# Agent attention with a maxout network behind it: the first product moved ahead of the first scores, own orders for the last four groups, the last store in two halves

## The chip, the cores and the metric

One core of a Trainium2 chip. The metric is the device time of one execution of the kernel in microseconds (us), the median over several runs. The five engines of the core work side by side, each through its own list of instructions in order, and wait for each other by semaphores: PE (TensorE, matrix products; PEld is its loading of the stationary operand), DVE (VectorE), ACT (ScalarE), POOL (GpSimd) and SP (SyncE, which here only starts transfers). PE writes into PSUM, a small memory from which DVE and ACT fetch the results.

## The reference

`q`, `k` and `v` have 4 batches of 12,544 rows with 128 columns; `agents` has 4 batches of 49 rows. All inputs and the output are 32-bit floats.

```python
def _attn_ref(q, k, v, agents):
    scale = 1.0 / np.sqrt(q.shape[-1])

    def sm(a, b):
        s = scale * (a @ b.transpose(0, 2, 1))
        s = s - s.max(-1, keepdims=True)
        e = np.exp(s)
        return e / (e.sum(-1, keepdims=True) + 1e-09)
    a2k = sm(agents, k)
    agent_v = a2k @ v
    q2a = sm(q, agents)
    return (q2a @ agent_v).astype(np.float32)

def _moe_ref(x, w1, w2, w3, w_out):
    h = np.maximum(np.maximum(x @ w1, x @ w2), x @ w3)
    return (h @ w_out).astype(np.float32)
```

The second function gets the first one's result as 50,176 rows of 128 columns; `w1`, `w2`, `w3` are 128x768 and `w_out` is 768x128.

## The kernel before

**What is multiplied with what.** The agents gather from `k` and `v` a 49x128 matrix `agent_v` per batch. The kernel multiplies it with the differences `w2 - w1` and `w3 - w1` (and a linear remainder) once per batch. The result `G` has 49 rows (kept twice, on partitions 0 to 48 and 64 to 112) and 1,792 columns: 768 at `C21`, 768 at `C31`, and two times 128 at `C1O`, of which one is the linear part. After that a group of rows of `q` needs only its scores against the 49 agents and products with `G` and `w_out`.

**Two kinds of groups.** A k group takes nine tiles of 128 rows of `k` and `v` of one batch (`k_group`). The k groups of batch 0 run first, alone, in the start ("early"); those of the later batches are fitted in between the q groups. A q group (`q_group`) takes eight tiles of 128 rows of `q`; there are `NQ = 49` of them, numbered 0 to 48. The steps of q group `s`, by the names that the order uses:

- `qt`, `qe`: turn `q` so that its columns lie on partitions (by PE and a copy, or in the last batch by a transposing transfer from SP); `s`: scores on PE (L507); `ex`: their exponential on ACT (L513) into `e_q`; `ho`: a PSUM tile for small sums; `sum` (L521) and `rec` (L527): one over the row sums.
- For each of six blocks `f` of 128 hidden columns: `u` (L533, PE, product with the `C31` part of `G`), `a` (relu on ACT, L548), `v` (L533, PE, product with the `C21` part), `x` (maximum of both on DVE, L558, into the tile `r`). Block 3 (`FI`) differs: its relu stays in PSUM (L545), `v3` adds onto it, and `x3` is a relu on ACT (L556).
- For each half `o` of the group's rows: `lin` (L563, PE), then for every `f` the step `oc` (L572, PE, four matmuls of `r` with `w_out`), and `sc` (L579, DVE: the PSUM tile times one over the row sums, into `o_sb`). `oc13` is half 1, block 3.
- `store` (L586): one transfer of 512 KB from SP's queue, after both `sc`.

**The order is written by hand.** Every step is handed to `at` (L119) with a key, a number; `emit` (L125) sorts all steps by key and writes them out. A step whose needs are not yet written, or for which no buffer is free, is held back until they are. Every engine then runs its own instructions in exactly that order. A q group's keys are `6.0 * s` plus an entry of a table: `KEY` for groups while k groups are still mixed in, `LATE` for the groups of the last batch, `BORDER` and `BEGIN` around the change of a batch (L101). Large negative numbers in a table only mean "as soon as the needs allow".

**Rings.** PSUM is shared out as three tiles of two banks (`uv`: hidden products, transposes of `k`, the products that make `G`) and two of one bank (`om`: everything else). The step that takes a tile waits for the reader of the tile that had its place.

**The start.** After the last k group of batch 0, `k_tail(0, ...)` (L382) has DVE write `avT`, the normalised `agent_v` (L402, L403), and `product` (L408) multiplies it with `wall`, the weight differences, on PE (L421), 64 output partitions at a time, and copies the result into `G` on DVE (L426). For batch 0 the first call makes 256 columns from `C31` and, in the other bank of the same PSUM tile, the next 512; the second call makes the 768 columns from `C21` in another tile. A matmul into a tile waits for the copy that still reads from it. In the order before, the steps stand so: two matmuls that only keep PE busy (`keep_busy`), `s` and `ex` of group 0, both products, the transposes of group 0's k rows (L294, from a cast on POOL, L280), their copy (L300), `u0`, `u1`, fillers, `v0` and so on. The scores `s` of group 0 wait for ACT's copy of `qT` (L494).

Of the kernel before, what the change touches and what calls it, by code (L numbers as in the profile page):

```python
# [11 lines left out]
AF = mybir.ActivationFunctionType  # L12
# [4 lines left out]
def kernel(  # L17
# [18 lines left out]
    nc = tc.nc  # L36
    B, N, C = q.shape
# [3 lines left out]
    P = 128  # L41
    NF = Dff // P
    H = 64
# [52 lines left out]
        "oc11": 11.381, "oc13": 11.497,  # L96
    }
    PRODUCT_KEYS = (-8.717, -1.818)
    BEHIND = 2.6

    def table(s):  # L101
        if s + 1 in tails:
            return BORDER
        return BEGIN if s in tails and s < SB else KEY if s < SB else LATE
# [6 lines left out]
    def uv_tile(dtype=FP32):  # L111
        return psum.tile([P, 2, 512 if dtype == FP32 else 1024], dtype, tag="uv", bufs=3, name="uv_ps")
# [6 lines left out]
    def at(key, fn, name=None, needs=(), ring=None, frees=()):  # L119

        ops.append((key, len(ops), fn, name, needs, ring, frees))
# [258 lines left out]
    def k_tail(b, sum_key, keys, s):  # L382
        d = {}

        def reduce():
            w = KT // 2 * A
            t = Eacc[b]
            while w >= A:
                nc.gpsimd.tensor_tensor(out=t[:, :w], in0=t[:, :w], in1=t[:, w:2 * w], op=ALU.add)
                w = w // A // 2 * A  # L390
            nc.gpsimd.tensor_tensor(out=e_sum[:, :A], in0=t[:, :A], in1=t[:, KT * A - A:], op=ALU.add)

        def total():
            for h in range(2):
                nc.tensor.matmul(host[s][h * H:(h + 1) * H, :1], e_sum, ones[:, :1], start=True,
                                 stop=True, skip_group_check=True)

        def normalise():
            if s is None:

                r = last_tile["t"][:, :A]
                nc.vector.reciprocal(r, Vacc[b][:, A:])  # L402
                nc.vector.tensor_tensor(out=avT[:, b, :A], in0=Vacc[b][:, :A], in1=r, op=ALU.mult)  # L403
            else:
                nc.vector.reciprocal(r_ag[:, b:b + 1], host[s][:, :1])
            G[b] = work.tile([P, WC], BF16, tag="G", name="G")

        def product(c0, *ends):  # L408

            t = uv_tile().rearrange("p i c -> p (i c)")  # L410

            at0 = c0 if len(ends) == 1 else ends[0] - 512
            a = c0
            for z in ends:
                cuts = sorted({a, z} | {c for c in (at0 + 512, C1O) if a < c < z})
                for lo, hi in zip(cuts, cuts[1:]):
                    for h in range(2):


                        c = lo + (C if lo >= C1O and h == 0 else 0)  # L420
                        nc.tensor.matmul(t[h * H:(h + 1) * H, lo - at0:hi - at0], avT[:, b, :],  # L421
                                         wall[:, c:c + hi - lo], start=True, stop=True,
                                         skip_group_check=True)
                src = t[:, a - at0:z - at0]
                if s is None:
                    nc.vector.tensor_copy(out=G[b][:, a:z], in_=src)  # L426
                else:
                    nc.scalar.activation(G[b][:, a:z], src, AF.Copy, scale=r_ag[:, b:b + 1])
                a = z

        if s is not None:
            at(6.0 * (s - 1) + table(s - 1)["ke"] + 1.51, reduce, ("sum_e", b), [("kx", s - 1)])
            at(sum_key + 0.8, total, ("total", s), [("sum_e", b), ("ho", s)])
        at(sum_key + 0.81, normalise, ("normalise", b),
           [("ka", ("early", NT - last_size))] if s is None else [("total", s), ("ka", s - 1)])

        pieces = ((C31, C31 + 2 * P, C1O) if s is None else (C31, WC), (C21, C31))
        for i, piece in enumerate(pieces):
            at(keys[i], lambda piece=piece: product(*piece),
               ("product", b, i), [("normalise", b)], "uv", [("product", b, i)])  # L440


    def split(t0, t1, step):
# [10 lines left out]
    def q_group(s):  # L454
# [120 lines left out]
        def out_scale(o):  # L575
            if "out" not in d:
                d["out"] = work.tile([P, GT, C], FP32, tag="o_sb", bufs=3, name="o_sb")
            j, m = 2 * pairs[o][0], 2 * len(pairs[o])
            nc.vector.tensor_tensor(  # L579
                out=d["out"][:, j:j + m, :],  # L580
                in0=d["o", o].rearrange("p (j c) -> p j c", c=C),
                in1=d["r"][:, j:j + m].unsqueeze(2).to_broadcast([P, m, C]), op=ALU.mult)
# [53 lines left out]
        for o in range(2):  # L636
            put(f"lin{o}", lambda o=o: out_linear(o), ("ex", s), *new_linear, ring="om",
                frees=[(f"sc{o}", s)])
            for f in range(NF):
                put(f"oc{o}{f}", lambda o=o, f=f: out_hidden(o, f), (f"lin{o}", s), (f"x{f}", s))  # L640
            put(f"sc{o}", lambda o=o: out_scale(o), ("rec", s),
                *[(f"oc{o}{f}", s) for f in range(NF)], *([("store", s - 3)] if s >= 3 else []))
        at(key + 12.2, store, ("store", s), [("sc0", s), ("sc1", s)])

    def ramp():

# [22 lines left out]
    for g, n in enumerate(first_sizes):  # L669
        k_group(0, sum(first_sizes[:g]), n, first_key + 6.0 * g, None)  # L670

        if 4 <= g < len(first_sizes) - 3:
            fillers += [(first_key + 6.0 * g + 0.55, 3), (first_key + 6.0 * g + 1.3, 3)]
    k_tail(0, last_key, (last_key + 0.95, last_key + 1.02), None)
    for key, n in fillers + [(last_key + 0.9, 2), (KEY["u1"] + 0.01, 2),
                             (KEY["u3"] + 0.05, 2)]:
        at(key, lambda n=n: keep_busy(n), ("busy", key), (), "om", [("busy", key)])
# [45 lines left out]
```

## Time and profile before

| what | value |
|---|---|
| median of 3 runs | 463.16 us (463.14 to 463.19) |
| the profiled execution's own time | 462.84 us |
| its span, first to last instruction | 461.0 us |
| distance of the stores of groups 44, 45, 46 (issued at 431.44, 439.30, 447.16) | 7.86 us |
| last store: issued, landed | 457.46, 460.07 us |
| one maximum on DVE (L558), mean of 245 | 1.220 us |
| one relu on ACT (L548), mean of 245 | 1.027 us |
| one scaling on DVE (L579), mean of 98 | 0.688 us |
| one output matmul on PE (L572), mean of 2,352 | 0.220 us from start to end; the next one starts earlier |

All times inside the profile are in microseconds from the start of the span. A row of the timeline gives start, duration, engine, line, operation, the tiles `out<-in`, shapes, and in brackets how long the engine was idle before it and who released it. Matmuls overlap: a row of 24 matmuls that takes 1.50 us is 1.35 us of the chain, and the rest is the last one's way through the array. In the stretch from 436.6 to 444.4, which is steady, PE was busy 7.77 of 7.80 us, ACT 7.27 and DVE 7.23. In the last stretch, from 452.3 to 461.0, PE was busy 4.20 of 8.70, DVE 3.71 and ACT 0.15.

The profile covers one execution; the runs of the table are others of the same kernel.

### The profile page before, as it was taken

How to read it: one execution, taken by the hardware profiler on the slowest of the kernel's cores; microseconds unless marked ns; L12 is line 12 of the kernel's file. 1: busy time of each engine (PE TensorE's matmuls, PEld its weight loads, DVE VectorE, ACT ScalarE, POOL GpSimd, SP SyncE). 2: the span in 40 equal slices, each digit the busy share in tenths (PEclk: the TensorE clock that was granted, in tenths of full speed). 3: DMA queues.
4: the chain of work that ended last, by engine and by line, in shares of the span. 5: the costliest groups of instructions: out<-in, count | busy, mean ns of one | idle time of the engine just before them, and what ended most of it. 6: DMA issues, size and time to landing. Idle time of an engine off the chain costs nothing.

```text
span 461.0 us, 13320 instructions
## 1 busy us (share of the span) xinstructions
PE 436.1 (95%) x5457; PEld 273.5 (59%) x5462; DVE 402.2 (87%) x510; ACT 396.6 (86%) x460; POOL 171.6 (37%) x179
## 2 busy tenths in 40 slices
PE   2597899999999999999999999999999999999996
PEld 2465456666656666666656666666656555555554
DVE  3255899999989999999989999999988999999995
ACT  3365989899899899898998998999999999999982
POOL 3235964644362536445273355363240101100000
PEclk9999999999999999999999999999999999999999
DMA  8999999999998999988998999997766465644122
GB/s 327 408 410 392 345 346 354 337 342 255 310 315 286 286 261 339 286 268 248 276 351 268 287 314 291 279 280 180 167 151 178 129 198 149 176 122 125 60 94 91
DMA packets 82632, 118.53 MB, mean 257 GB/s; under 512 B 56391, under 2 KB 57867, under 8 KB 82571
## 3 DMA queue, kind: packets, MB, share of 16 engines
q1 hardware_dynamic: 82368, 117.59, 84.8%
q8 instruction: 42, 0.69, 0.6%
q14 instruction: 19, 0.16, 0.1%
q10 hardware_dynamic: 203, 0.10, 0.1%
HBM read 78.74 MB, written 25.69 MB: 227 GB/s over the span
## 4 chain that ended last, share of the span: by engine, by line
PE 81%; DMA 8%; DVE 5%; ACT 4%; issue 1%; SPq 0%; POOL 0%; DVEq 0%; ACTq 0%
PE uv_ps L533 34%; PE o_ps L572 29%; PE o_ps L563 6%; DMA st<-in_k_dram 5%; PE m_ps L486 4%; DVE r L558 4%; PE m_ps L507 3%; ACT a_sb L548 2%; DMA st<-in_q_dram 2%; DMA st<-in_v_dram 2%; PE m_ps L323 2%; PE m_ps L312 1%; PE m_ps L521 1%; DVE o_sb L579 0%; DVE G L426 0%
## 5 line engine op out<-in xcount | busy, mean ns | idle before, releaser
L558 DVE TENSOR_TENSOR r<-uv_ps,a_sb 128x1024 bf16<-128x1024 f32 x245 | 297.3, 1220 | 16.3 <-PE uv_ps L533 7.6
L548 ACT ACTIVATE a_sb<-uv_ps 128x1024 bf16<-128x1024 f32 x245 | 240.8, 1027 | 15.4 <-PE uv_ps L533 13.9
L533 PE MATMUL uv_ps<-e_q,G 49*128 49x512 bf16 (+3 forms) x1248 | 186.8, 368 | 2.6 <-DVE G L426 0.4
L572 PE MATMUL o_ps<-wo_bf,r 128*128 128x128 bf16 x2352 | 175.2, 220 | 0.2 <-DVE r L558 0.2
L572 PEld LDWEIGHTS <-r 128*128 128x128 bf16 x2352 | 137.8, 98 | 40.1 <-issue 38.1
L533 PEld LDWEIGHTS <-G 49*128 49x128 bf16 x1248 | 57.7, 93 | 64.7 <-issue 32.9
L342 POOL TENSOR_TENSOR Eacc<-Eacc,e_k 128x441 f32<-128x441 f32 (+1 forms) x30 | 30.5, 1015 | 124.9 <-ACT e_k L317 124.9
L579 DVE TENSOR_TENSOR o_sb<-o_ps,recips 128x512 f32<-128x512 f32 x98 | 67.5, 688 | 9.1 <-PE o_ps L572 6.3
L481 POOL CAST q_bf<-st 128x1024 bf16<-128x1024 f32 x49 | 51.0, 1043 | 62.0 <-DMA qT<-q_bf 59.2
L556 ACT ACTIVATE r<-uv_ps 128x1024 bf16<-128x1024 f32 x49 | 50.2, 1024 | 18.0 <-PE uv_ps L533 17.7
L280 POOL CAST k_bf<-st 128x1152 bf16<-128x1152 f32 (+2 forms) x45 | 50.4, 1120 | 28.6 <-DMA st<-in_k_dram 26.4
L545 ACT ACTIVATE uv_ps<-uv_ps 128x1024 f32<-128x1024 f32 x49 | 49.6, 1012 | 0.2
L563 PE MATMUL o_ps<-G,e_q 128*128 128x256 bf16 x196 | 38.0, 276 | 0.0
L287 POOL CAST v_bf<-st 128x1152 bf16<-128x1152 f32 (+1 forms) x33 | 37.5, 1136 | 0.9 <-ACT e_q L513 0.6
L513 ACT ACTIVATE e_q<-m_ps 128x512 bf16<-128x512 f32 x49 | 29.8, 608 | 0.5 <-PE m_ps L507 0.5
L285 ACT ACTIVATE v_bf<-st 128x1152 bf16<-128x1152 f32 (+1 forms) x12 | 12.9, 1074 | 13.9 <-DMA st<-in_v_dram 13.9
L563 PEld LDWEIGHTS <-e_q 128*128 128x128 bf16 x196 | 12.5, 97 | 18.7 <-issue 18.0
L300 DVE COPY kT<-uv_ps 128x1152 bf16<-128x1152 bf16 (+1 forms) x14 | 9.9, 708 | 14.8 <-PE uv_ps L294 14.8
L486 PEld LDWEIGHTS <-q_bf 128*128 128x128 bf16 x264 | 14.9, 98 | 13.0 <-issue 11.1
L492 DVE COPY qT<-m_ps 128x1024 bf16<-128x1024 bf16 x32 | 21.8, 680 | 0.0
L486 PE MATMUL m_ps<-ident,q_bf 128*128 128x128 bf16 x264 | 20.4, 220 | 0.4 <-POOL q_bf L481 0.4
L507 PE MATMUL m_ps<-qT,agT 128*64 128x512 bf16 (+3 forms) x104 | 19.9, 388 | 0.7 <-ACT qT L494 0.7
(71 smaller groups left out, 224.9 us busy)
## 6 DMA issues: line engine op xcount, KB each, us to landing
st<-in_q_dram SPq DMA_DIRECT2D x46, 512.0 KB, 5.2
out_dram<-o_sb SPq DMA_DIRECT2D x46, 512.0 KB, 3.8
st<-in_k_dram SPq DMA_DIRECT2D x40, 576.0 KB, 6.7
st<-in_v_dram SPq DMA_DIRECT2D x40, 576.0 KB, 7.9
st<-in_k_dram SPq DMA_DIRECT2D x3, 512.0 KB, 8.0
st<-in_v_dram SPq DMA_DIRECT2D x3, 512.0 KB, 6.8
wst<-in_moe_w_dram SPq DMA_DIRECT2D x3, 384.0 KB, 10.7
st<-in_q_dram SPq DMA_DIRECT2D x2, 384.0 KB, 4.9
```

Source lines behind the costliest of these rows:

```text
L280: nc.gpsimd.tensor_copy(out=d["kb"][:, :n, :], in_=d["k"][:, :n, :])
L287: nc.gpsimd.tensor_copy(out=d["vb"][:, :n, :], in_=d["v"][:, :n, :])
L481: nc.gpsimd.tensor_copy(out=d["qb"], in_=d["q"])
L486: nc.tensor.transpose(t[:, j * P:(j + 1) * P], d["qb"][:, j, :], ident)
L533: nc.tensor.matmul(t[:, h, j0 * P:j1 * P], G[b][h * H:h * H + A, col + f * P:col + (f + 1) * P], d["e"][h * H:h * H + A, j0 * P:j1 * P], s ...
L545: nc.scalar.activation(u, u, AF.Relu)
L548: nc.scalar.activation(a_sb[f], u, AF.Relu)
L556: nc.scalar.activation(r, v_ps[f], AF.Relu)
L558: nc.vector.tensor_tensor(out=r, in0=v_ps[f], in1=a_sb[f], op=ALU.max)
L563: nc.tensor.matmul(t[:, i * 2 * C:(i + 1) * 2 * C], d["e"][:, jj * P:(jj + 1) * P], G[batch[jj]][:, C1O:C1O + 2 * C], start=(i == 0), stop ...
L572: nc.tensor.matmul(t[:, c:c + C], r_sb[f][:, h, jj * P:(jj + 1) * P], wo_bf[:, f, :], start=False, stop=True, skip_group_check=True)
L579: nc.vector.tensor_tensor(out=d["out"][:, j:j + m, :], in0=d["o", o].rearrange("p (j c) -> p j c", c=C), in1=d["r"][:, j:j + m].unsqueeze( ...
```

## The change

Three things change. All else, and the order of groups 1 to 44, stays as it was.

1. The products of batch 0 come as three steps. The first makes 256 columns from `C31` (one PSUM tile, first bank). The second, in a tile of its own, makes the next 512 columns of `C31` and the first 512 of `C21`, with two copies. The third makes the last 256 columns of `C21` in the second bank of the first tile, so it waits for the first copy. The first two are keyed ahead of `s` of group 0, the third behind it. The products of batches 1 to 3 keep their two pieces.
2. Groups 45 to 48 get a table each (`LAST`) in place of `LATE`. As written out, the end of the lists then reads: on DVE `x4` of group 48, `sc0` of group 47, `x5` of group 48, `sc0` of group 48 (before: `x4`, `x5`, `sc0` of 47, `sc1` of 48, `sc0` of 48); on PE, behind `x5`, the steps `oc15`, `oc05`, `oc02`, four matmuls each (before: `oc15`, `oc13`, `oc12`, `oc11`, `lin0` and all six `oc0`).
3. Of group 48, the half `o = 1` is scaled on ACT, by four instructions of 128x128, and stored from ACT's queue; the half `o = 0` is scaled on DVE as before and stored from SP's queue. Each store is 256 KB, 2 KB per partition.

```diff
     PRODUCT_KEYS = (-8.717, -1.818)
+    LAST = [
...
+        {"a4": -135.5952, "s": -3.6850, "ex": -2.2030, "ho": -1.9346, "u0": -1.3390,
...
+         "oc05": 60.1508, "lin0": 70.3912, "oc03": 74.0752, "oc00": 92.6315, "oc01": 97.6449,
+         "x5": 102.3830, "oc02": 107.1067},
+    ]
     def table(s):
+        if s >= NQ - len(LAST):
+            return LAST[s - NQ]
...
+        def multiply(t, at0, a, z):
+            cuts = sorted({a, z} | {c for c in (a - at0 + 512, C1O) if a < c < z})
+            for lo, hi in zip(cuts, cuts[1:]):
+                for h in range(2):
+                    c = lo + (C if lo >= C1O and h == 0 else 0)
+                    nc.tensor.matmul(t[h * H:(h + 1) * H, at0 + lo - a:at0 + hi - a], avT[:, b, :],
+                                     wall[:, c:c + hi - lo], start=True, stop=True,
+                                     skip_group_check=True)
...
+        cut = C31 + 2 * P
+        def product_first():
+            t = d["p"] = uv_tile().rearrange("p i c -> p (i c)")
+            multiply(t, 0, C31, cut)
+            nc.vector.tensor_copy(out=G[b][:, C31:cut], in_=t[:, :cut - C31])
+        def product_second():
+            t = uv_tile().rearrange("p i c -> p (i c)")
+            multiply(t, 0, cut, C1O)
+            multiply(t, 512, C21, C21 + 512)
+            nc.vector.tensor_copy(out=G[b][:, cut:C1O], in_=t[:, :C1O - cut])
+            nc.vector.tensor_copy(out=G[b][:, C21:C21 + 512], in_=t[:, 512:])
+        def product_third():
+            multiply(d["p"], 512, C21 + 512, C31)
+            nc.vector.tensor_copy(out=G[b][:, C21 + 512:C31], in_=d["p"][:, 512:512 + C31 - C21 - 512])
...
+        if s is None:
+            at(keys[0], product_first, ("product", 0, 0), [("normalise", 0)], "uv", [("product", 0, 2)])
+            at(keys[0] + 0.001, product_second, ("product", 0, 1), [("product", 0, 0)], "uv",
+               [("product", 0, 1)])
+            at(keys[1], product_third, ("product", 0, 2), [("product", 0, 0)])
...
+            if s == NQ - 1 and o == 1:
+                for i in range(m):
+                    nc.scalar.activation(d["out"][:, j + i, :], d["o", o][:, i * C:(i + 1) * C], AF.Copy,
+                                         scale=d["r"][:, j + i:j + i + 1])
+                return
...
-        at(key + 12.2, store, ("store", s), [("sc0", s), ("sc1", s)])
+        def store_half(o):
+            queue = nc.scalar if o else nc.sync
+            j, m = 2 * pairs[o][0], 2 * len(pairs[o])
+            dst = out[s * GT * P:(s + 1) * GT * P, :].rearrange("(p j) c -> p j c", j=GT)
+            queue.dma_start(dst[:, j:j + m, :], d["out"][:, j:j + m, :])
+        if s < NQ - 1:
+            at(key + 12.2, store, ("store", s), [("sc0", s), ("sc1", s)])
+        else:
+            for o in range(2):
+                at(key + 120, lambda o=o: store_half(o), ("store", s, o), [(f"sc{o}", s)])
...
-    k_tail(0, last_key, (last_key + 0.95, last_key + 1.02), None)
+    k_tail(0, last_key, (last_key + 0.93, last_key + 1.02), None)
```

## The prediction

> **What bounds the kernel now.** I read the page's header and shares first, then the chain that ended last with its pieces in time, then the timeline of the two stretches that the diff touches.
>
> ```profile
> span 461.0 us, 13320 instructions
> ...
> PE 436.1 (95%) x5457; PEld 273.5 (59%) x5462; DVE 402.2 (87%) x510; ACT 396.6 (86%) x460; POOL 171.6 (37%) x179
> ...
> PE 81%; DMA 8%; DVE 5%; ACT 4%; issue 1%; SPq 0%; POOL 0%; DVEq 0%; ACTq 0%
> ```
>
> PE is the bound of the body. From 63 us to 445 us nearly every piece of the chain is a PE piece, and the SP rows issue the stores of groups 44, 45 and 46 at 431.44, 439.30 and 447.16, one group per 7.86 us. The change leaves the order of groups 1 to 44 alone, so there is nothing to gain in the body; a shift made before it arrives at its end. What can move lies at the two ends, where the chain leaves PE. The start first (pieces of the chain: start, us, what; then rows of the timeline):
>
> ```profile
> 42.08 1.03 ACT qT L494
> 43.11 0.04 issue
> 43.16 0.41 PE m_ps L507 x2
> 43.56 0.12 PE uv_ps L421 x2
> 43.69 0.02 issue
> 43.71 0.43 DVE G L426
> 44.14 0.04 issue
> 44.19 0.42 PE uv_ps L421 x2
> 44.61 0.02 issue
> 44.63 1.56 DVE G L426 x2
> 46.20 0.04 issue
> 46.24 0.39 PE uv_ps L533 x2
> ```
>
> ```profile
> 43.30 1.15 POOL L280 CAST k_bf<-st 128x1152 bf16<-128x1152 f32 x1 [1.94 <-DMA st<-in_k_dram]
> ...
> 44.85 0.68 PE L294 MATMUL uv_ps<-ident,k_bf 128*128 128x128 bf16 x9
> ...
> 45.46 0.39 PE L533 MATMUL uv_ps<-e_q,G 49*128 49x512 bf16 x2
> ...
> 45.89 1.94 ACT L548 ACTIVATE a_sb<-uv_ps 128x1024 bf16<-128x1024 f32 x2 [1.69 <-PE uv_ps L533]
> ```
>
> The product G, a PE and DVE ping-pong, begins only after the scores that wait for qT, although its operand avT is written at 42.34 (the DVE row of L403: 42.13 for 0.21). The second matmul of group 0 waits for the last copy into G until 46.24. Then the end:
>
> ```profile
> 451.67 2.36 DVE L558 TENSOR_TENSOR r<-uv_ps,a_sb 128x1024 bf16<-128x1024 f32 x2 [0.39 <-PE uv_ps L533]
> ...
> 454.08 1.07 PE L572 MATMUL o_ps<-wo_bf,r 128*128 128x128 bf16 x16 [0.21 <-DVE r L558]
> ...
> 455.20 1.50 PE L572 MATMUL o_ps<-wo_bf,r 128*128 128x128 bf16 x24
> 456.75 0.69 DVE L579 TENSOR_TENSOR o_sb<-o_ps,recips 128x512 f32<-128x512 f32 x1 [0.87 <-PE o_ps L572]
> ```
>
> Here the last r is done at 454.03, PE then has 40 output matmuls and a linear pair left, and one scaling and one store of 512 KB stand behind them. The store is issued at 457.46 and lands at 460.07.
>
> **The start, step by step.** Moved: the first product's two 256-column matmuls, before the scores. They need avT (42.34 + 0.05) and the fillers' end (42.48): start 42.48. The DVE copy followed such a pair by 0.34 (43.37 to 43.71), so it runs from 42.82 to 43.24. The second step has its own PSUM tile and four matmuls of 512 columns, two at a time, 0.21 a pair (44.19 to 44.40): it ends about 43.05, before qT at 43.10, so the scores start at 43.16 as now and the exponential at 43.60. DVE then copies 512, 512 and 256 columns instead of 512 and 768. Its rows are 0.42 for 256 and 1.55 for 512 and 768 back to back, so about 0.26 for each 256 more: 0.66, 0.66 and 0.42, until 45.0 instead of 46.19. The fourth copy instruction costs DVE 0.2 (2.16 against 1.97 in all), covered because DVE starts 0.89 earlier. The third product waits for the first copy (43.24); behind it on PE stand the transposes of group 0's k, which cannot start before POOL's cast is done anyway (43.30 + 1.15 = 44.45). So they start at 44.50, not 44.85: 0.35 earlier. The first hidden matmul follows 0.61 later (44.85 to 45.46): 45.11, and ACT's first relu at 45.54 against 45.89. DVE's first maximum gains more, about 0.85, because the second hidden pair no longer waits until 46.24.
>
> Which one counts is ACT: from 45.89 its rows run on to 49.49 with 0.14 us of idle time, so the later steps keep ACT's gain, not DVE's. What is late next is POOL (casts of the next groups end at 47.00 and 48.87), whose consumers on PE start at 48.08 and 50.62, so it has room for the shift. I take **0.35**. Ends: 0.2, if the third copy (until 45.0 plus its signal) and the first relu collide and half the gain goes; 0.55, if the shorter wait for the second transposes (they waited 0.54 for DVE, which gains more than ACT) is passed on. No SP or POOL instruction moves here.
>
> **The end.** The own tables put the last group's remaining work before its last maximum. In the new order DVE ends with maximum 4, scaling of group 47, maximum 5, one scaling of group 48; PE has three blocks of four matmuls left after maximum 5. From maximum 5 to the end of the last scaling, now: 457.44 - 454.03 = 3.41. Then: 0.05 to PE, 12 matmuls (1.07 for 16, less four at 0.056 from 1.35 for 24 = 0.85), 0.04, 0.69 = 1.63. Saved 1.78. Paid: group 47's scaling, 0.69, now stands ahead of maximum 5. Against it, DVE's idle rows before that point (0.37 at 445.24, 0.39 at 451.67) can close; maximum 5 still needs ACT's and PE's rows, both over 90% busy, so I close a third, 0.25. Net 1.78 - 0.69 + 0.25 = **1.35**. Ends: 1.85 with all 0.76 closed; 0.5 with none closed and a new stall like DVE's 0.57 before 455.19.
>
> ACT's scaling of the other half replaces one DVE instruction of 0.69 by four of 128x128. The nearest row is L240, 0.27 for 128x128, so 4 x 0.27 = 1.08. It starts after maximum 5 and the first of the three blocks (0.05 + 0.39 + 0.04) and is done at 1.56, beside DVE's 1.63: no cost while it ends first; if each took 0.4 as L249's 256 columns do, 0.45 later than DVE. On ACT nothing is behind it but its store; its queue of semaphore waits is for stores landed 14 us before (group 45's).
>
> **The store.** The last store took 2.60 us from issue to landing, and the five before 2.61 to 2.90. In the packet records its 128 packets of 4,096 bytes took 160 ns each, eight per DMA engine: 1.28, leaving 1.32 around it. 2,048-byte packets, as the halves make, took 84 ns: eight are 0.67. Alone, the last half would land in 1.99, gain 0.6. Together both halves take 1.32 + 1.34 = 2.66 from the first issue; with ACT's half issued 0.1 to 0.2 ahead that is **0.1** gained. Lower end -0.3: the one earlier issue on ACT's queue took 0.57 against 0.34 on SP's. That load was used 4.3 us after its issue, beside 4.04 for SP's load issued at the same moment, so the queue itself is not slow.
>
> [...]
>
> **Sum.** 0.35 + 1.35 + 0.1 = 1.8. The profiled execution took 462.84, of which 461.0 is span; 1.84 around it stays. So its span becomes 459.2 and its time 461.04. The median of the runs is 463.16, 0.32 above the profiled one; with the same difference the forecast is **461.36**.
>
> **Rivals.** (a) The start's gain is absorbed: transposes and relus are set by casts and loads that don't move. For it, POOL's idle 1.94 for a DMA before 43.30; against it, the 0.35 is counted from that very cast. Time 461.7. (b) The new orders of groups 45 to 48 lose between the groups what they save at the end: PE, DVE and ACT are 99%, 93% and 93% busy there, so an order that suits the end can leave PE waiting. For it, the trace's own irregular orders: over a border two groups took 17.87 us (stores at 132.11 and 149.98) against 16.70, so 1.17 more, of which 0.75 or so is product work. Losing one such 1.17 gives 463.16 - 1.8 + 1.17 = 462.5, no change by this measurement. (c) Slower: the same stall in three of the four groups, 3 x 1.17 = 3.5, gives 464.9; it decides from two groups on (1.8 / 1.17 = 1.5). Against both, the border orders have a product in them and these don't, and every instruction of these groups is one that the steady order has too.
>
> **How the numbers follow.** Forecast 0.68 (its own range 460.8 to 462.0), (a) 0.12, (b) 0.12, (c) 0.08. About 0.2%, 0.93 us, is what a measurement of this kernel can tell from no change. Forecast and (a) are faster by more, (b) within it, (c) slower: 0.80, 0.12, 0.08. The range: the upper ends of the three terms together are 3.0 and the lower 0.4; all three seldom fall together, so 2.6 to 0.7 saved, 460.6 to 462.5, which takes in (a) and touches (b).
>
> **What would show it.** Right: the first product matmul starts near 42.5, the first relu near 45.5, the body's chain 0.35 earlier (group 42's store near 415.4 instead of 415.72); the last DVE scaling ends near 455.75, 1.6 after the last L558; two store issues within 0.3 us, the last landing 2.3 to 2.6 after the first. Wrong: a body shifted by nothing or by over 0.6; group periods over 8 us after 430; ACT's four scalings ending well after DVE's; the ACT store landing later than 3 us after issue.

## The result and the profile after

| | before | after |
|---|---|---|
| median, on the same chip | 463.18 us (463.14 to 463.34, 4 runs) | 461.83 us (461.79 to 461.94, 4 runs) |
| ratio after to before | | 0.9971, 95% interval 0.9953 to 0.9988 |
| distance of the stores of groups 43 to 47 | 7.86, 7.86, 7.87, 7.48 us | 7.86, 7.86, 7.44, 6.49 us |
| last maximum ends, last scaling ends | 454.49, 457.90 us | 454.66, 456.31 us |
| last store issued, landed | 457.93, 460.54 us | 456.35, 459.05 us |

Faster by 1.35 us, 0.3%. The forecast was 461.36. The time rows of "before" are from a second profile of the unchanged kernel (463.26 in the median of its own runs, span 461.5), since the first profile turns out to be an early execution: the load of group 0's q lands at 40.27 us in it and at 40.67 in the second, and everything behind is 0.4 later. In the other twelve profiles of this study it lands between 40.53 and 40.81, in the changed kernel's at 40.53. Comparisons below are with the second profile, and the lines of the changed kernel stand 35 to 63 further down than before: L421 is L456, L280 is L320, L294 is L334, L533 is L590, L548 is L605, L558 is L615, L572 is L629 and L579 is L642.

The page of the changed kernel (span; busy time by engine; the chain's shares):

```profile
span 460.0 us, 13331 instructions
...
PE 436.4 (95%) x5462; PEld 273.9 (60%) x5462; DVE 401.4 (87%) x510; ACT 397.6 (86%) x464; POOL 171.5 (37%) x179
...
PE 82%; DMA 8%; DVE 3%; ACT 3%; issue 1%; POOL 0%; SPq 0%; DVEq 0%; ACTq 0%
```

PE still bounds the body. DVE's share of the chain falls from 5% to 3%: the ping-pong at the start and the scalings at the end are what went. The start, as pieces of the chain of waits (start, us, what):

```profile
42.30 0.43 PE m_ps L294 x2
42.73 0.66 PE uv_ps L456 x6
43.40 0.02 issue
43.41 0.42 PE m_ps L564 x2
43.84 0.07 issue
43.91 1.16 POOL k_bf L320
45.07 0.05 issue
45.11 0.68 PE uv_ps L334 x9
45.79 0.54 PE uv_ps L590 x4
```

The six product matmuls (L456) stand ahead of the scores (L564), and no copy into G is on the chain any more. In its place stands a piece that wasn't there: POOL's cast of k, then the transposes that need it. The end, as rows of the timeline:

```profile
452.85 0.68 DVE L642 TENSOR_TENSOR o_sb<-o_ps,recips 128x512 f32<-128x512 f32 x1
453.44 1.21 DVE L615 TENSOR_TENSOR r<-uv_ps,a_sb 128x1024 bf16<-128x1024 f32 x1
...
453.86 1.73 PE L629 MATMUL o_ps<-wo_bf,r 128*128 128x128 bf16 x28
455.18 1.14 ACT L639 ACTIVATE o_sb<-o_ps,recips 128x128 f32<-128x128 f32 x4 [2.19 <-PE o_ps L629]
455.62 0.69 DVE L642 TENSOR_TENSOR o_sb<-o_ps,recips 128x512 f32<-128x512 f32 x1 [0.96 <-PE o_ps L629]
456.34 0.33 SPq L710 DMA_DIRECT2D out_dram<-o_sb  x1
456.35 0.38 ACTq L710 DMA_DIRECT2D out_dram<-o_sb  x1
```

Only three blocks of four matmuls are left behind the last maximum; both scalings end at the same moment, and so both stores start at the same moment. Where the end's time came from is in the busy times of the stretch 445 to 453 us (length, then busy time and instructions of each engine, clock, DMA). First the unchanged kernel:

```profile
445.00:453.00 8.00, 7.53 (x79) 4.19 (x77) 7.19 (x9) 6.58 (x7) 0.00 (x0) 1.00 0.18 70
```

Then the changed one:

```profile
445.00:453.00 8.00, 7.97 (x99) 5.47 (x97) 7.44 (x10) 6.54 (x7) 0.00 (x0) 1.00 0.18 70
```

PE's work at the end is the same in both kernels; the new orders do 20 matmuls more of it before 453, so that less stands behind the last maximum.

### The profile page after: what moved, and what is told of

Its sections match the earlier page's. It is cut to its first block, busy times and chain, and to the rows that moved or that the text cites. A ratio compares the mean times of both kernels' runs of the same rounds, so it can differ in the third digit from the quotient of the medians.

```text
span 460.0 us, 13331 instructions
## 1 busy us (share of the span) xinstructions
PE 436.4 (95%) x5462; PEld 273.9 (60%) x5462; DVE 401.4 (87%) x510; ACT 397.6 (86%) x464; POOL 171.5 (37%) x179
## 4 chain that ended last, share of the span: by engine, by line
PE 82%; DMA 8%; DVE 3%; ACT 3%; issue 1%; POOL 0%; SPq 0%; DVEq 0%; ACTq 0%
PE uv_ps L590 35%; PE o_ps L629 30%; PE o_ps L620 6%; DMA st<-in_k_dram 5%; PE m_ps L543 4%; PE m_ps L564 3%; DVE r L615 3%; ACT a_sb L605 2%; DMA st<-in_q_dram 2%; DMA st<-in_v_dram 2%; PE m_ps L363 2%; PE m_ps L352 1%; PE m_ps L578 1%; ACT e_q L570 0%; ACT G L463 0%
## 5 line engine op out<-in xcount | busy, mean ns | idle before, releaser
L615 DVE TENSOR_TENSOR r<-uv_ps,a_sb 128x1024 bf16<-128x1024 f32 x245 | 297.1, 1219 | 16.8 <-PE uv_ps L590 7.8
L605 ACT ACTIVATE a_sb<-uv_ps 128x1024 bf16<-128x1024 f32 x245 | 241.1, 1027 | 14.0 <-PE uv_ps L590 12.6
L590 PE MATMUL uv_ps<-e_q,G 49*128 49x512 bf16 (+3 forms) x1248 | 186.9, 368 | 1.8 <-ACT a_sb L605 0.4
L629 PE MATMUL o_ps<-wo_bf,r 128*128 128x128 bf16 x2352 | 175.5, 220 | 0.0
L629 PEld LDWEIGHTS <-r 128*128 128x128 bf16 x2352 | 137.7, 98 | 40.7 <-issue 39.1
L590 PEld LDWEIGHTS <-G 49*128 49x128 bf16 x1248 | 57.9, 93 | 64.1 <-issue 32.1
L642 DVE TENSOR_TENSOR o_sb<-o_ps,recips 128x512 f32<-128x512 f32 x97 | 66.7, 688 | 8.5 <-PE o_ps L629 5.6
L320 POOL CAST k_bf<-st 128x1152 bf16<-128x1152 f32 (+2 forms) x45 | 50.5, 1121 | 29.1 <-DMA st<-in_k_dram 23.1
L334 PE MATMUL uv_ps<-ident,k_bf 128*128 128x128 bf16 x116 | 11.2, 255 | 9.8 <-POOL k_bf L320 8.5
```

Of the source, the lines that this page charges most:

```text
L320: nc.gpsimd.tensor_copy(out=d["kb"][:, :n, :], in_=d["k"][:, :n, :])
L590: nc.tensor.matmul(t[:, h, j0 * P:j1 * P], G[b][h * H:h * H + A, col + f * P:col + (f + 1) * P], d["e"][h * H:h * H + A, j0 * P:j1 * P], s ...
L605: nc.scalar.activation(a_sb[f], u, AF.Relu)
L615: nc.vector.tensor_tensor(out=r, in0=v_ps[f], in1=a_sb[f], op=ALU.max)
L629: nc.tensor.matmul(t[:, c:c + C], r_sb[f][:, h, jj * P:(jj + 1) * P], wo_bf[:, f, :], start=False, stop=True, skip_group_check=True)
L642: nc.vector.tensor_tensor(out=d["out"][:, j:j + m, :], in0=d["o", o].rearrange("p (j c) -> p j c", c=C), in1=d["r"][:, j:j + m].unsqueeze( ...
```

## The experiments

Some of these kernels start from the kernel before, the others from the changed one. Differences are always to the kernel before on the same chip, because its median was 463.19 to 463.43 on different chips.

### Each part alone

The unchanged kernel once more, as the yardstick:

> The kernel before unchanged, a second profile of it, to see how much of a difference between two profiles is chance. If the 0.3 us by which the first q load landed later in the changed kernel's profile, and the 0.4 us that its body lost between groups 8 and 24, are chance, then this profile differs from the first one by similar amounts, up to 0.4 us, at the start or in the body; if they belong to the changed kernel, this profile agrees with the first within 0.1 at every group.

Measured: 463.26 (463.17 to 463.45), ratio 1.0000 (0.9991 to 1.0009). The later landing of q is chance by it (40.67); the loss between groups 8 and 24 is the changed kernel's, for their exponentials are 135.58 apart there, and 135.25 here and 135.23 in the first profile.

Part 1 alone, the products in the start:

```diff
+            at(keys[0], product_first, ("product", 0, 0), [("normalise", 0)], "uv", [("product", 0, 2)])
+            at(keys[0] + 0.001, product_second, ...
+            at(keys[1], product_third, ("product", 0, 2), [("product", 0, 0)])
...
-    k_tail(0, last_key, (last_key + 0.95, last_key + 1.02), None)
+    k_tail(0, last_key, (last_key + 0.93, last_key + 1.02), None)
```

> The kernel before with only the products of batch 0 in three steps, two of them ahead of the first scores. Theory (the changed kernel's gain is nearly all at the end; at the start the first relu hangs on POOL's cast of group 0's k rows, and so on the landing of that load): 0.0 to 0.4 us saved, and in the profile the first relu follows the end of that cast by 1.1 us as it does in the changed kernel (45.06 to 46.16), with a group 1 exponential 0.1 to 0.4 earlier than in the kernel before. Rival (the product's place is worth the forecast 0.35 in every run and the profile of the changed kernel lost it by chance): 0.35 saved or a little more.

Measured: 462.67 (462.32 to 463.00), ratio 0.9988 (0.9979 to 0.9997), 0.58 less, more than the theory's 0.4. The first relu follows the cast's end by 1.09, as expected; group 1's exponential is 0.54 earlier, not 0.1 to 0.4. Where the 0.58 comes from is told further down.

Part 2 alone, the tables of the last four groups:

```diff
     def table(s):
+        if s >= NQ - len(LAST):
+            return LAST[s - NQ]
```

> The kernel before with only the own tables of groups 45 to 48; the last group is scaled on DVE twice and stored in one piece from SP. Theory (the order alone brings the end's gain, the scaling on ACT keeps it from being given back): maximum 5 ends about 0.7 later than before, then both scalings stand behind each other on DVE, so the last scaling ends 0.4 to 0.7 later than in the changed kernel: 0.7 to 1.1 us saved. Rival (ACT's scaling costs as much as it spares, 1.14 us on ACT against 0.69 on DVE): 1.3 to 1.5 saved.

Measured: 461.96 (461.79 to 462.17), ratio 0.9972 (0.9962 to 0.9982), 1.29 less, more than the theory's 1.1 and nearly the rival's 1.3: the last maximum ends only 0.32 later than before, not 0.7. DVE's two last scalings run back to back and end 1.80 after the last maximum instead of 3.41; the one store takes 2.61 to land.

Part 3 alone, ACT's scaling and the two stores, in the old order:

```diff
+            if s == NQ - 1 and o == 1:
+                for i in range(m):
+                    nc.scalar.activation(...)
...
+                at(key + 120, lambda o=o: store_half(o), ("store", s, o), [(f"sc{o}", s)])
```

> The kernel before with only the last group's half 1 scaled on ACT and the two half stores; order of the groups as before. In that order half 1 is done 1.5 us before half 0, so its store is under way when half 0 is done. Theory (the half store is worth something only if the halves are staggered): the last half store lands about 2.0 after its issue instead of 2.6, 0.5 to 0.7 us saved. Rival (two stores cost what one does, the fixed part decides): 0.0 to 0.2 saved.

Measured: 462.60 (462.49 to 462.78), ratio 0.9986 (0.9977 to 0.9995), 0.65 less. The rows show why this is much more than in the changed kernel:

```profile
455.71 1.14 ACT L620 ACTIVATE o_sb<-o_ps,recips 128x128 f32<-128x128 f32 x4 [2.74 <-PE o_ps L610]
455.73 1.50 PE L610 MATMUL o_ps<-wo_bf,r 128*128 128x128 bf16 x24
456.89 0.38 ACTq L691 DMA_DIRECT2D out_dram<-o_sb  x1
457.27 0.69 DVE L623 TENSOR_TENSOR o_sb<-o_ps,recips 128x512 f32<-128x512 f32 x1 [2.12 <-PE o_ps L610]
457.99 0.33 SPq L691 DMA_DIRECT2D out_dram<-o_sb  x1
```

In the old order ACT's half is ready 1.1 us ahead of DVE's. Each half then has the transfer engines to itself (the packets of the first end at 458.59, those of the second begin at 458.82): they land 2.05 and 2.01 after their issues, against 2.61 for one store.

The three parts bring 0.58, 1.29 and 0.65 alone, 2.52 in sum, and 1.35 together. Two questions follow: what happened to part 3, and what to part 1.

### Parts 2 and 3 without part 1

The changed kernel with the old product order.

```diff
-            at(keys[0], product_first, ...
+        pieces = ((C31, C31 + 2 * P, C1O) if s is None else (C31, WC), (C21, C31))
```

> The changed kernel without the part in the start: old product order, own orders for the last four groups, scaling on ACT and the last store in halves. Theory (in the new order the two halves end together, so the store in halves adds nothing to the orders): about as the orders alone, 461.85 to 462.0, with the last landing about 2.7 us after the issue. Rival (the parts add up, 1.29 and 0.65): 461.3.

Measured: 461.80 (461.68 to 462.51), ratio 0.9971 (0.9961 to 0.9982), 1.39 less. The halves go together at 456.40 and land after 2.37 and 2.68. So beside the new orders part 3 is worth 0.1 (1.39 against 1.29), which is less than the spread of either run. The second reading is the more important one: with part 1 taken out, the changed kernel is as fast as with it, 461.80 against 461.83. **Part 1 is worth nothing in the full change, though it brings 0.58 alone.**

### Where part 1 went

Part 1 does arrive in the body. The start of the exponentials of a few groups:

| group | before, second profile | after | difference |
|---|---|---|---|
| 1 | 52.98 | 52.49 | -0.49 |
| 8 | 111.95 | 111.48 | -0.47 |
| 9 | 120.31 | 119.96 | -0.35 |
| 23 | 234.94 | 234.64 | -0.30 |
| 24 | 247.20 | 247.06 | -0.14 |
| 44 | 409.25 | 409.11 | -0.14 |

Of the 0.49, 0.35 is lost, 0.28 of it in two steps, from group 8 to 9 and from 23 to 24, though the change doesn't touch these groups. Both lie on DVE. Rows of DVE in the unchanged kernel, near 111, 240 and 445 us:

```profile
110.60 0.69 DVE L579 TENSOR_TENSOR o_sb<-o_ps,recips 128x512 f32<-128x512 f32 x1
111.27 3.91 DVE L558 TENSOR_TENSOR r<-uv_ps,a_sb 128x1024 bf16<-128x1024 f32 x3
...
239.85 2.54 DVE L558 TENSOR_TENSOR r<-uv_ps,a_sb 128x1024 bf16<-128x1024 f32 x2 [0.44 <-PE uv_ps L533]
...
445.70 1.23 DVE L558 TENSOR_TENSOR r<-uv_ps,a_sb 128x1024 bf16<-128x1024 f32 x1 [0.36 <-PE uv_ps L533]
```

The same three places in the changed kernel:

```profile
110.13 0.69 DVE L642 TENSOR_TENSOR o_sb<-o_ps,recips 128x512 f32<-128x512 f32 x1
111.16 3.55 DVE L615 TENSOR_TENSOR r<-uv_ps,a_sb 128x1024 bf16<-128x1024 f32 x3 [0.34 <-PE m_ps L564]
...
239.90 2.35 DVE L615 TENSOR_TENSOR r<-uv_ps,a_sb 128x1024 bf16<-128x1024 f32 x2 [0.79 <-PE uv_ps L590]
...
445.21 1.23 DVE L615 TENSOR_TENSOR r<-uv_ps,a_sb 128x1024 bf16<-128x1024 f32 x1
```

Two waits of about 0.35 have come, and one of 0.36 is gone. The named releasers don't explain them, since PE's work for these maxima stands in the same order in both kernels. The trace also has DVE's wait instructions: at the second place in the changed kernel the one ahead of the maximum ends at 239.50, ACT's last signal came at 239.37, and the maximum starts at 239.90; in the unchanged kernel that wait instruction ends at 239.80 and the maximum starts at 239.85. What is common shows when DVE's instructions are numbered in the order in which the trace has them (from 1, wait instructions counted too). The waiting maxima are number 192 and 448 in the changed kernel and 832 in the kernel before. Part 1 has four copies in the start where there were three, so every later DVE instruction stands one place further on. Without part 1 the numbers 192 and 448 aren't computing instructions at all; with part 1, 832 isn't a maximum. All three numbers are 64 modulo 128.

That is a guess from a pattern until the numbering is moved with nothing else. First, the kernel before with one constant set twice, ahead of the body:

```diff
     nc.vector.memset(sel, 0.0)
+    nc.vector.memset(sel, 0.0)
```

> The kernel before with one DVE memset doubled ahead of the body (sel is set to zero twice) and nothing else, so that every later DVE instruction stands one place further on in DVE's program. Theory (the waits belong to places in the program): DVE idles 0.34 before the maximum near 111.5 and 0.79 before the one near 240.3, which the kernel before doesn't, and the wait of 0.36 before the maximum at 445.7 is gone; time 463.1 to 463.3, since the two effects nearly cancel. Rival (the waits come from the new start): the idle times are those of the kernel before at all three places.

Measured: 463.13 (463.04 to 463.27), ratio 0.9999 (0.9990 to 1.0007). Its DVE rows:

```profile
110.49 0.69 DVE L580 TENSOR_TENSOR o_sb<-o_ps,recips 128x512 f32<-128x512 f32 x1
111.53 3.54 DVE L559 TENSOR_TENSOR r<-uv_ps,a_sb 128x1024 bf16<-128x1024 f32 x3 [0.35 <-PE m_ps L508]
...
240.22 2.36 DVE L559 TENSOR_TENSOR r<-uv_ps,a_sb 128x1024 bf16<-128x1024 f32 x2 [0.79 <-PE uv_ps L534]
...
445.51 1.23 DVE L559 TENSOR_TENSOR r<-uv_ps,a_sb 128x1024 bf16<-128x1024 f32 x1
```

All three waits change as the theory has it, with the start untouched. The exponentials lose 0.13 from group 8 to 9 and 0.16 from 23 to 24, and the stretch from group 44's exponential to the end of the last maximum is 44.90 instead of 45.24. One instruction that does nothing moves three waits, and their sum happens to be near zero.

This also explains the 0.58 that part 1 brings alone. In that run's profile group 44's exponential is 0.27 earlier (408.98 against 409.25), and from there to the end of the last maximum it takes 44.89 instead of 45.24: 0.35 of the gain is the wait at 445, gone with the shift. The new orders move that maximum too (it is number 830 with the orders alone, 831 in the changed kernel), so the full change can't gain this 0.35 a second time.

Then the other way round: the changed kernel, with another constant set by POOL instead of DVE, so that the numbering is the old one.

```diff
-    nc.vector.memset(ones, 1.0)
+    nc.gpsimd.memset(ones, 1.0)
```

> The changed kernel, with one memset of constants ahead of the body (ones) moved from DVE to POOL, so that DVE's program has as many instructions before each maximum as the kernel before. [...]

Measured: 461.20 (461.03 to 461.44), ratio 0.9957 (0.9945 to 0.9970), 1.99 less than before. Waits that follow the numbering were expected to give 461.5 to 461.75, and waits that come from the new start 461.83; the time is 0.3 below the first range. Its DVE rows at the two places:

```profile
110.61 3.91 DVE L615 TENSOR_TENSOR r<-uv_ps,a_sb 128x1024 bf16<-128x1024 f32 x3
...
239.18 2.54 DVE L615 TENSOR_TENSOR r<-uv_ps,a_sb 128x1024 bf16<-128x1024 f32 x2 [0.44 <-PE uv_ps L590]
```

The waits are gone, and the gain of group 1 (52.31, 0.67 early) is still there at group 44 (408.54, 0.71 early). The time falls by 0.63 against the changed kernel. The profiles account for 0.30 of it by the two waits and for 0.18 by POOL's cast of k, which began at 43.73 here and at 43.91 there; the rest isn't attributed. A wait of 0.36 was expected to come back near 445 and doesn't, because in the new orders number 832 isn't a maximum with either numbering. Against the run without part 1 (461.80, same numbering, same chip) part 1 is now worth 0.60.

### What sets the start

The thirteen profiles follow one rule each for the old and the new start. In the six with the old order, group 1's exponential begins 12.30 or 12.31 after group 0's q has landed. In the seven with the new order (the next experiment apart) it begins 8.58 after POOL begins the cast of group 0's k, and the first relu 2.24 or 2.25 after it. In all fourteen profiles that cast begins 0.14 or 0.15 after its load of k has landed (43.76 and 43.91 in the changed kernel, though the chain names PE's scores there). The change moves the gate of the start from the q load to the k load. Its worth is so 12.30 - 8.58 = 3.72, less what lies between q's landing and the cast's start in that execution: 2.92 to 3.49, so 0.23 to 0.80, and 0.34 in the profiled run of the changed kernel (3.38). The 0.49 of the table is this 0.34 and the 0.14 by which q landed earlier in that execution (40.53 against 40.67). So the 0.14 left at group 44 isn't the change's: its own 0.34 is all lost on the way.

If the cast is the gate, then the first hidden product shouldn't stand behind k's transposes. In this run they change places on PE (on top of the run with the old numbering):

```diff
-                turn = 2.7 if s else last_key + 1.05
+                turn = 2.7 if s else KEY["u1"] + 0.005
```

> The changed kernel with the memset of ones on POOL (so without the two waits of DVE), and with the transposes of group 0's k put behind the first hidden product of group 0 on PE instead of ahead of it; nothing else differs, and only PE's order changes. Theory (what gates the start after the change is POOL's cast of k, 43.7 to 44.9, through these transposes): the first hidden product starts when the exponential is done, near 44.8 instead of 45.54, the first relu near 45.25 instead of 45.97, and the body and the time come up to 0.7 earlier, 460.5 to 461.0. Rival (the next link, DVE's copies into G or kT being late, takes the gain): 461.1 to 461.3.

Measured: 461.89 (461.84 to 461.99), ratio 0.9968 (0.9956 to 0.9981), 1.54 less, so 0.45 worse than the run it is built on, and worse than theory and rival. ACT's rows:

```profile
43.90 0.60 ACT L570 ACTIVATE e_q<-m_ps 128x512 bf16<-128x512 f32 x1 [0.49 <-PE m_ps L564]
44.98 1.94 ACT L605 ACTIVATE a_sb<-uv_ps 128x1024 bf16<-128x1024 f32 x2 [0.48 <-PE uv_ps L590]
48.54 1.01 ACT L602 ACTIVATE uv_ps<-uv_ps 128x1024 f32<-128x1024 f32 x1 [1.62 <-issue]
```

The theory is right about its first link and wrong about the sum. The first relu comes a full microsecond earlier (44.98 against 45.97), and two relus later ACT idles 1.62, so that the third one is 0.74 late (48.54 against 47.80). In the order written out one pair of hidden products now falls behind the transposes of the next group's q on PE; that this is for want of a free PSUM tile, since the transposes of k take theirs later, is a reading and wasn't tried. Group 1's exponential is 0.54 later, at 12.28 behind q's landing: the gain of part 1 is undone.

### What sets the last store

The same kernel (part 1, new orders, old numbering) without part 3, one scaling on DVE behind the other and one store:

```diff
-            if s == NQ - 1 and o == 1:
+            if False:
...
+        at(key + 12.2, store, ("store", s), [("sc0", s), ("sc1", s)])
```

> The changed kernel with both last scalings on DVE and one store of 512 KB again, and the memset of ones on POOL as in the run above: the part in the start and the orders alone. Theory (the halves are worth 0.05 in the new order, the DVE places 0.1 to 0.3): 461.45 to 461.75, the last store lands 2.6 after its issue. Rival (the halves are worth the 0.65 that they bring alone): 462.1 or more.

Measured: 461.31 (461.21 to 461.76), ratio 0.9961 (0.9948 to 0.9973), 1.88 less, a little below the theory's range. From the end of the last maximum to the landing it takes 4.44; with part 3 4.37. ACT's scaling saves 0.16 and the two stores cost 0.09 more than one.

ACT's scaling kept, one store:

```diff
+        at(key + (120 if s == NQ - 1 else 12.2), store, ("store", s), [("sc0", s), ("sc1", s)])
```

> The changed kernel with the memset of ones on POOL and the scaling of one half on ACT, but one store of 512 KB from SP behind both scalings instead of two halves from two queues. Theory (issued together, the halves are no faster than one store): the store lands 2.6 after its issue where the halves landed in 2.69, and the time is 461.1 to 461.2. Rival (two queues carry more than one): it lands later than the halves do, 461.3 or more.

Measured: 461.29 (461.21 to 461.36), ratio 0.9955 (0.9942 to 0.9967), 2.14 less; the store lands 2.61 after its issue, 4.32 after the last maximum. (The expectation was counted from a chip on which the kernel before takes 463.19, and comes to 1.99 to 2.09 less.) Two halves issued together bring nothing over one store.

The halves apart: DVE scales the half that PE finishes first and SP stores it, the other half is shared by ACT and DVE.

```diff
-            if s == NQ - 1 and o == 1:
-                for i in range(m):
+            if s == NQ - 1 and o == 0:
+                for i in range(2, m):
...
-            queue = nc.scalar if o else nc.sync
+            queue = nc.sync if o else nc.scalar
```

> The changed kernel with the memset of ones on POOL, and the last group's scalings shared in another way: the half that PE finishes first (at 454.55) is scaled by DVE in one instruction of 0.69 and stored from SP, the other half by ACT (two of 0.285) and DVE (256 columns) side by side and stored from ACT. Theory (two halves issued together take 2.7 to land, one alone 2.0, so the stagger decides and not the queues): first issue 0.45 before that of the run with the memset moved, the last issue 0.1 before, 0.3 to 0.4 apart, the last landing 2.2 to 2.4 after its issue; time 0.35 to 0.5 lower than 461.2, 460.7 to 460.85. Rival (the landing of the last half doesn't depend on the distance of the issues): 2.7 after its issue, 461.1.

Measured: 461.12 (460.97 to 461.65), ratio 0.9952 (0.9939 to 0.9966), 2.31 less.

```profile
454.82 0.69 DVE L645 TENSOR_TENSOR o_sb<-o_ps,recips 128x512 f32<-128x512 f32 x1 [0.52 <-PE o_ps L629]
455.27 0.62 ACT L638 ACTIVATE o_sb<-o_ps,recips 128x128 f32<-128x128 f32 x2 [2.63 <-PE o_ps L629]
455.54 0.33 SPq L713 DMA_DIRECT2D out_dram<-o_sb  x1
455.93 0.42 DVE L640 TENSOR_TENSOR o_sb<-o_ps,recips 128x256 f32<-128x256 f32 x1 [0.41 <-ACT o_sb L638]
456.38 0.38 ACTq L713 DMA_DIRECT2D out_dram<-o_sb  x1
```

The halves land 2.01 and 2.06 after their issues. The sharing failed, though: DVE waited 0.41 for ACT before it took its part of the same PSUM tile, so the two ran one after the other and the issues are 0.84 apart instead of 0.35. The landing comes 4.14 after the last maximum, and the time is a little short of what was expected (from the 463.19 it was counted from, 2.34 to 2.49 less). So sharing isn't needed, and DVE can do both:

```diff
-            if s == NQ - 1 and o == 1:
+            if False:
...
-            queue = nc.scalar if o else nc.sync
+            queue = nc.sync if o else nc.scalar
```

> The changed kernel with the memset of ones on POOL, both last scalings on DVE, one behind the other as in the run without halves, and the last group stored in halves: the half that DVE scales first from SP, the other from ACT. Theory (what the last store takes is decided by the distance of the two issues, and ACT's scaling only brought them together): DVE's scalings end 1.15 and 1.83 after the last maximum, the issues are 0.65 apart, each half lands 2.0 to 2.1 after its issue, the last landing 3.9 to 3.95 after the last maximum's end instead of 4.37 (the run with the memset moved) and 4.44 (the run without halves); time 460.65 to 460.85. Rival (the run with shared scalings gained only because of its distance of 0.84, and 0.65 leaves the halves in each other's way): the last half lands 2.4 or more after its issue and the time is 461.1 or more.

Measured: 461.14 (460.93 to 461.31), ratio 0.9953 (0.9939 to 0.9966), 2.22 less.

```profile
453.09 1.21 DVE L615 TENSOR_TENSOR r<-uv_ps,a_sb 128x1024 bf16<-128x1024 f32 x1
...
454.82 1.29 DVE L642 TENSOR_TENSOR o_sb<-o_ps,recips 128x512 f32<-128x512 f32 x2 [0.52 <-PE o_ps L629]
455.54 0.33 SPq L710 DMA_DIRECT2D out_dram<-o_sb  x1
456.15 0.38 ACTq L710 DMA_DIRECT2D out_dram<-o_sb  x1
```

The issues are 0.61 apart, the halves land after 2.05 and 2.09, and the last landing is 3.93 after the last maximum, as the theory has it. The time is less clear, and short of the theory's range: 0.23 better than the run with ACT's scaling where the profile promises 0.44; the body was 0.2 later in this run's profile. This and the run before it, 2.2 to 2.3 less than the kernel before, are the fastest of the study; between the two the spreads don't decide. Nor do they settle the gain over one store behind both scalings: that run is 2.14 less, so the medians give 0.17 and 0.08, where the profiles show 0.18 and 0.39 from the last maximum to the landing.

## Why the prediction came out as it did

Its sum was 0.35 + 1.35 + 0.1 = 1.8; the medians differ by 1.35, and the two profiled spans by 1.48 (461.49 to 460.01): 0.14 in the body, 1.45 from there to the end of the last scaling, and -0.09 for the store, the rest rounding. The 0.14 is the earlier landing of q; without it the three parts are 0, 1.45 and -0.09, which comes to the 1.35 of the medians within 0.01. The end was sized well; the miss is in the start (0.35) and the store (0.19), and the end gives 0.1 back.

**The start: the first link was right, what is kept was wrong, and the loss wasn't foreseen.** The products ran at 42.66 (42.5 forecast), and the first relu follows the cast by 2.24, which is what the forecast's 45.54 was counted from. But the first relu near 45.5 was tied to one execution's cast at 43.30; here it began at 43.91 and the relu at 46.16. The step that failed first is "the later steps keep ACT's gain, not DVE's". From the first relu to group 1's exponential the old order takes 6.68 or 6.69 in five of its profiles and 6.58 in the one with the latest cast, and the new one 6.33 or 6.34: group 1's exponential starts 3.22 or 3.23 after DVE's second maximum begins in all thirteen, and that maximum is 3.11 behind the first relu in the new order, 3.46 (once 3.35) in the old. So DVE's gain is passed on as well. In the forecast's own execution part 1 would have been worth 12.30 + 40.27 - 8.58 - 43.30 = 0.69, twice the 0.35. The bounds of 0.2 to 0.55 named this case and put it too low. Against it stands the loss: the two waits that a fourth copy brings 66 and 195 us later, 0.30. "The fourth copy instruction costs DVE 0.2, covered" was costed by its duration alone; what it costs is a place in DVE's program. The body came 0.14 earlier at group 44, and the store of group 42 at 416.04 against 416.17.

**The end: right, with one term right for another reason.** From the last maximum to the end of the last scaling it is 1.65 us (454.66 to 456.31; forecast 1.63) after 3.41. ACT's four scalings took 1.14 (forecast 1.08) and end with DVE's, at no cost. The net is 1.45 (forecast 1.35). The step "I close a third, 0.25" of DVE's idle rows came out as 0.38: group 47's scaling takes 0.69, but from group 44's exponential to the end of the last maximum it is only 0.31 more (45.55 after 45.24). This isn't the closing that was meant: the idle row of 0.37 at 445.24 was the wait at number 832, which a shift of DVE's numbering takes away, 0.35 by the run with the doubled constant; that the term came out near its size is luck. Beside a kernel without that wait, scaling 47 ahead of maximum 5 costs 0.65 of its 0.69 (45.55 from group 44's exponential to the end of the last maximum, against 44.90). So of the 1.45 only about 1.1 come from the orders and ACT's scaling. The other idle row, 0.39, didn't close: the changed kernel has one of 0.47 at 448.68.

**The store: sized by a stagger that didn't exist.** The forecast took ACT's half to be issued 0.1 to 0.2 ahead. Both scalings ended at the same moment, the issues are 0.01 apart, and the last half lands after 2.70 where one store took 2.61. That lies within the range that was given (down to -0.3). The last landing comes 2.71 after the first issue, outside the 2.3 to 2.6 that were named as the sign of being right. The forecast's number for a half alone, 1.99, was right: 2.01 to 2.09 in six landings. In the changed kernel two queues at the same moment gained nothing, 2.70 against 2.61, and one store behind the same scalings did as well. What shortened the landing was the distance of the issues. Whether it needs a second queue at all wasn't tried.

**The rivals.** (a), the start's gain absorbed, at 461.7, is nearest to the measured time, and its effect is what the run without part 1 shows. The first relu does hang on the cast, as (a) says, but a gain of 0.34 got past the cast, and it was the waits in DVE's program that took most of it. (b) and (c) fell: the distances of the stores in the new groups are 7.86, 7.86, 7.44 and 6.49, nowhere longer than before.

## What to carry to other kernels

One instruction more on an engine that feeds the bound can cost more than its duration, far from where it stands (here 0.30 for a copy costed at 0.2, in two waits 66 and 195 us later): compare the drift of a marker (here each group's exponential) over the whole body, and before reading a gain of some tenths, shift the engine's program by one harmless instruction and see what that alone does. The start was gated by a load: q's in the old order, k's in the new one, where POOL's cast begins 0.14 or 0.15 after the landing. When a load lands differs from one execution to the next (q's at 40.27 to 40.81 in these profiles), so price a gain there from several profiles, relative to the landing. A half of the last store landed sooner when the two issues were apart (2.01 to 2.09 after its issue, against 2.68 to 2.70 when they were within 0.01), and two queues alone brought nothing (2.70 against 2.61 for one store); so scale and send the half that is ready first instead of balancing the engines to end together. Here that shows in the landings, while the gain in time is within the spreads.

## What the runs showed of the hardware

**A wait at places of DVE's program.** Maxima at number 192, 448 and 832 of DVE's program waited 0.34 to 0.37 longer in every profile where they stood there (three profiles each), and not in those where the numbering was shifted by one. Other instructions showed no such wait: the copy at 320 and the scaling at 832 in the changed kernel have none at all. What a maximum has that these lack isn't settled. The DMA records have packets of 8,192 bytes of the kind "instruction" on queue 14 within 3 us of each such place, for example at 113.80, 241.63 and 446.12 in the changed kernel; whose instructions these are isn't shown by the records. At all three places the packet starts after the late maximum (at 113.80 and 241.63 against 111.16 and 239.90, and in the kernel before at 446.29 against 445.70), so the maximum didn't wait for that packet. What it waited for stays open.

**How long a store takes depends on its neighbour.** At the very end of the kernel 256 KB landed 2.01 to 2.09 after the issue when the other 256 KB were issued 0.6 us or more apart; issued within 0.01 of each other, the later one landed after 2.68 to 2.70; 512 KB in one store took 2.60 or 2.61. The packets show the difference: in the changed kernel those of the two halves run side by side, from 457.17 to 458.35 and from 457.51 to 458.69, 1.18 each, where a half alone takes 0.83 (457.76 to 458.59 with part 3 alone).
